# Attention and two expert layers on one core: gate rows of batch 0 in float32r from tiles of their own, later stacks in two tiles

## The chip, the cores and the metric

The kernel runs on one core of one Trainium2 chip. The metric is the time of one execution on the device in microseconds (us): the median of several runs. Lower is better. The engines are named as in the profile: PE is TensorE's matmul, PEld its weight load, DVE is VectorE, ACT ScalarE, POOL GpSimd and SP SyncE, which here only issues DMAs.

## The reference, cut to what matters

Attention over 4 batches of 8 heads, 576 positions and a head size of 64, with a causal mask and a bias from a running sum of `s`, and behind it two feed-forward layers on the 2304 tokens:

```python
scores = scale * np.matmul(q, k.transpose(0, 1, 3, 2))
s_pos = np.maximum(s, 0.0)
cum = np.cumsum(s_pos, axis=-1)
bias = -(cum[:, :, :, None] - cum[:, :, None, :])
scores = np.where(causal, -1000000000.0, scores + np.minimum(bias, 0.0))
attn = np.exp(scores - np.max(scores, axis=-1, keepdims=True))
attn = attn / (np.sum(attn, axis=-1, keepdims=True) + 1e-09)
out = np.matmul(attn, v)
# layer 1: h = x @ w_in; softmax of h times h; layer norm; @ w_out
# layer 2: h = x @ w_in; h * clip(h + 3, 0, 6) / 6; @ w_out
```

What matters here is the bias. It is a difference of two running sums, so a head's scores plus bias are one matrix product: the rows of q and k, and beside them four "gate rows" that hold the running sum in two parts (a float32r value and its rest) and ones.

## The kernel before, in words

**Tiling.** Two heads of a batch make a pair; pairs 0 to 3 are batch 0, pairs 4 to 15 the batches 1 to 3. Queries of a head are cut into five tiles t, of 128, 128, 128, 96 and 96 rows; a tile meets keys 0 to its own end, so its product is 128, 256, 384, 480 or 576 columns wide, the last as two pieces of 288. Each piece goes to one of eight PSUM banks, from there DVE (L525, with the mask and the row's minimum) writes it to SBUF, ACT takes the exponential (L537), POOL divides by the sum (L620, L638), PE transposes (L672), DVE or ACT copy back (L676) and PE multiplies with v (L701).

**Batch 0** (`qk_whole`, L577) runs in float32. For a tile it issues for both heads the product of the gate rows (m = 0) and then that of q and k (m = 1), each on 64 partitions, head 0 on partitions 0 to 63 and head 1 on 64 to 127. The gate rows lie in planes 2 and 3 of the tiles `whole0` and `whole1` (four planes of 576 columns; even pairs use `whole0`, odd ones `whole1`): rows 0 to 3 of each half hold gate rows, the others are zeros from one memset at the start (L286). Planes 0 and 1 take q and k of pairs 2 and 3; those of pairs 0 and 1 lie in `HL`. A pair's gate rows are loaded by `load_gates` (L421) from `rows_d`. Tiles 0 and 1 of all pairs come first (`pairs(False)`), then tiles 2 to 4 (`pairs(True)`).

**Batches 1 to 3** (`qk`, L604) run in float32r on 128 partitions, in two products a piece, from a stack per head parity (`stack0`, `stack1`, four planes): partitions 0 to 63 of planes 0 and 1 hold the high parts of q and k, partitions 64 to 127 of all four planes hold high and low parts, and rows 0 to 3 of planes 2 and 3 the gate rows. `to_stack` fills it by DMA on SP: for q and for k one copy of 64 x 576 (L485) and one of 64 x 2 x 576 (L486), then the gate rows (L489). A stack has one buffer, so the copies for a pair wait for the last product of that head parity in the pair before. The tags `stack0` and `stack1` first hold `whole0` and `whole1`; the stacks take their place, with a memset of planes 2 and 3 on POOL (L499).

**Around it.** PE also carries layer 1 (L806 with w_in, L872 the transposes, L893 with w_out) and, at the end, layer 2 (L1053, L1084). The weights come as float64 and are decoded on ACT, DVE and POOL between the steps of batch 0.

**The order.** Every step is added to a plan with an engine, a cost in us and what it reads and writes; the plan simulates the engines with these costs and gives each engine a fixed order. A cost in the plan is thus not a time on the chip but moves steps about, on every engine.

Of the kernel before, what the change touches and what calls it, by code (L numbers as in the profile page):

```python
# [184 lines left out]
def kernel(ctx, tc, q, k, v, s, w_in, w_out, g_ln, w2_in, w2_out, out):  # L185
    nc = tc.nc
# [71 lines left out]
    whole_t, stack_t = {}, {}  # L258
    nc.scalar.activation(out=nmax[:, 0, 0:1], in_=halfs, func=AF.Exp)

    def gate_rows():


        s_sb = ap2.tile([P, S], F32, tag="y4", name="s_sb")[:NH]
        one = ap2.tile([P, S], F32, tag="y4", name="one")[:NH]
        cum = ap2.tile([P, NQ, 2, D], F32, tag="V", name="cum").rearrange("p c j d -> p (c j d)")[:NH, :S]
        pos = ap2.tile([P, PT_COLS], F32, tag="pt", name="pos", bufs=PT).bitcast(F32R)[:NH, : 2 * S]
        neg = ap2.tile([P, PT_COLS], F32, tag="pt", name="neg", bufs=PT).bitcast(F32R)[:NH, : 2 * S]

        def load():  # L270
# [24 lines left out]
        for j in range(2):  # L295
            plan.add("POOL", 1.3, lambda j=j: zeros(j), writes=[f"zeros{j}"], new=[(f"stack{j}", 1, f"whole{j}")])

    def split64(plan, pool, src, hi, lo, name, key, scale=None, bufs=1, ring="", raws64=2, after=(), hi_dve=False, on_dve=(), behind=None):

# [112 lines left out]
            plan.add("SP", 0.5 + 0.5 * a, lambda j=j: values(j), writes=[f"{key}/{j}"], new=[("V", 2, key)] if j == 0 else [], lag=3.0, after=[begun(p)])  # L412

    def gates_at(p, j):
        return whole_t[p % 2][j * D : (j + 1) * D, 2:4, :]

    def load_gates(p, a):

        def gates():
            for j in range(2):  # L420
                nc.sync.dma_start(out=gates_at(p, j)[:4], in_=rows_d[2 * p + j].rearrange("i r s -> r i s"))  # L421

        plan.add("SP", 0.8, gates, reads=ROWS_D + [f"zeros{p % 2}", f"whole{p % 2}"], writes=[f"G{p}{a}"], new=[("G", 2, f"G{p}{a}")], lag=2.0)

    def prep_whole(p, name):

# [15 lines left out]

        if name == "q":
            load_gates(p, 0)
        ring = [("HL0", 2, hl_key)] if p < 2 else []
        home = [] if p < 2 else [f"zeros{p % 2}", f"whole{p % 2}"]
        for c0 in (0, 3):
            key = f"pp{p}{name}{c0}"
            plan.add("PE", 3 * 0.083, lambda c0=c0, key=key: turn(c0, key), reads=[raw_key, *home], writes=[key],
                     new=ring if name == "q" and c0 == 0 else [], bank=key, after=[] if name == "q" and c0 == 0 else [f"pp{p}q0"])  # L450
            plan.add(*(("ACT", act(3 * n)) if name == "q" else ("DVE", dve(3 * n))), lambda c0=c0, key=key: put(c0, key), reads=[key, *home], writes=[f"{hl_key}/{name}{c0}"])

    def prep_qk(p, name):
        if p < NPAIR:
# [42 lines left out]
        def zeros(j):  # L497
            stack_t[j] = ap1.tile([P, 4, S], F32R, tag=f"stack{j}", name=f"stack{j}")
            nc.gpsimd.memset(stack_t[j][:, 2:4, :].bitcast(F32), 0.0)  # L499

        def to_stack(j):
            if p == NPAIR and name == "q":
                plan.add("POOL", 1.3, lambda j=j: zeros(j), writes=[f"stack{j}/"], new=[(f"stack{j}", 1, f"stack{j}")])
            s_key = f"S{p}_{j}"
            plan.add("SP", 1.26, lambda j=j: stack(j), reads=[f"{hl_key}/{x}{c0}" for x in "hl" for c0, _ in groups] + [f"stack{j}/"],
                     writes=[f"{s_key}/{name}"], new=[(f"S{j}", 1, s_key)] if name == "q" else [], lag=3.0)
            if name == "k":
                plan.add("SP", 0.45, lambda j=j: gates(j), reads=ROWS_D + [f"stack{j}/"], writes=[f"{s_key}/g"], lag=2.0)
# [38 lines left out]
    def qk_whole(p, t):  # L547
# [32 lines left out]
        for c0, c1, at in pieces:  # L580
# [6 lines left out]
            plan.add("PE", 4 * max(0.07, 0.00033 * (c1 - c0)), lambda c0=c0, c1=c1, keys=keys: mm(c0, c1, keys),  # L587
                     reads=[f"HL{p}/{x}{c}" for x in "qk" for c in ((0, 3) if late else (0,))] + [f"G{p}{late:d}", f"whole{p % 2}"], writes=keys, new=new, bank=keys, after=[f"sc{heads[0]}_{t}_0"] if c0 else [])
# [6 lines left out]
    def qk(h, t):  # L595
# [587 lines left out]
```

## Time and profile before

| | |
|---|---|
| median of 3 runs | 851.12 us |
| lowest and highest | 850.43 and 853.88 us |
| the profiled execution | 855.06 us |
| its span | 853.1 us |
| PE busy | 822.0 us, 96% |
| DVE, ACT, POOL busy | 51%, 47%, 24% |
| L577, from first to last start | 15.2 to 90.4 us |
| L604, from first to last start | 98.4 to 362.5 us |
| shares of the chain that ended last, L577 and L604 | 3% and 5% |

The profile is one execution. Busy time of PE counts a matmul from its start to a modelled end, and matmuls overlap, so 96% does not say that PE is at its peak. A float32 product is two PE instructions in the trace. PEclk is the granted clock of TensorE as a share of 2.4 GHz; 0.50 is 1.2 GHz.

### The profile page before, as it was taken

What the parts mean: (1) busy time and instruction counts of PE and PEld (TensorE: products, weight loads), DVE (VectorE), ACT (ScalarE), POOL (GpSimd) and SP (SyncE); (2) the same over time, 40 slices, a digit from 0 to 9 for tenths busy, and PEclk for the clock granted to TensorE, in tenths of its full rate; (3) what the DMA queues carried; (4) which work ended last, traced back from release to release, by engine and by line L of the source; (5) the groups of instructions that cost most, each with busy time, mean ns of one, the idle gap of its engine ahead of it and who ended that gap; (6) DMA issues with size and microseconds to landing.
All of it is one profiled execution on the core that took longest, in us unless ns stands there. A gap on an engine that the chain in (4) does not pass through costs nothing.

```text
span 853.1 us, 13546 instructions
## 1 busy us (share of the span) xinstructions
PE 822.0 (96%) x4864; PEld 692.4 (81%) x4864; DVE 438.6 (51%) x1125; ACT 399.8 (47%) x928; POOL 206.0 (24%) x309
## 2 busy tenths in 40 slices
PE   3899999999999999998998999999999999999998
PEld 3565688988898889887897999998888888888886
DVE  4677887756756574658625894233222232222221
ACT  2575767756766566645534773243222322232222
POOL 1563644434533263335300221000000000000000
PEclk9899999999999999999999999999999999999999
DMA  6753596754556445243206660012000200010001
GB/s 171 179 148 110 126 210 148 174 129 109 127 138 136 101 103 123 63 136 107 86 32 202 203 219 1 0 62 87 1 0 1 87 13 0 1 50 1 0 1 50
DMA packets 95938, 77.52 MB, mean 91 GB/s; under 512 B 64288, under 2 KB 78112, under 8 KB 95872
## 3 DMA queue, kind: packets, MB, share of 16 engines
q1 hardware_dynamic: 93568, 68.27, 31.7%
q10 hardware_dynamic: 2304, 8.39, 3.0%
q8 instruction: 38, 0.62, 0.3%
q14 instruction: 28, 0.23, 0.1%
HBM read 45.38 MB, written 10.03 MB: 65 GB/s over the span
## 4 chain that ended last, share of the span: by engine, by line
PE 89%; DVE 4%; DMA 3%; POOL 2%; issue 1%; ACT 1%; SPq 0%; ACTq 0%; POOLq 0%; DVEq 0%
PE bank L1053 23%; PE bank L1084 23%; PE bank L893 11%; PE bank L806 10%; PE bank L701 6%; PE bank L672 5%; PE bank L604 5%; PE bank L577 3%; PE bank L872 2%; PE bank L467 1%; DMA raw_w2o<-in_moe_w_out_dram 1%; DMA stack<-HL12k 1%; POOL y L638 1%; DMA rows_d<-neg 1%; DVE y L525 0%
## 5 line engine op out<-in xcount | busy, mean ns | idle before, releaser
L1053 PE MATMUL bank<-x2h,w 128*128 128x512 f32 (+1 forms) x640 | 186.8, 373 | 0.5 <-ACT x2s L898 0.5
L1084 PE MATMUL bank<-w,gh 128*128 128x512 f32 x576 | 178.7, 393 | 2.1 <-ACT gh L1065 2.1
L1061 DVE SCALAR_TENSOR_TENSOR g<-g,bank 128x512 f32<-128x512 f32 (+1 forms) x80 | 50.6, 632 | 206.8 <-ACT g L1057 206.6
L1053 PEld LDWEIGHTS bank<-x2h,w 128*128 128x128 f32 x640 | 119.7, 189 | 19.4 <-ACT x2s L898 0.7
L1057 ACT ACTIVATE g<-bank 128x512 f32<-128x512 f32 (+1 forms) x80 | 44.4, 555 | 178.4 <-PE bank L1053 178.2
L1084 PEld LDWEIGHTS bank<-w,gh 128*128 128x128 f32 x576 | 107.9, 188 | 24.4 <-ACT gh L1065 2.5
L1053 PE MATMUL bank<-x2l,w 128*128 128x512 f32 (+1 forms) x320 | 119.1, 372 | 0.0
L1084 PE MATMUL bank<-w,gl 128*128 128x512 f32 x288 | 111.8, 392 | 0.0
L525 DVE CUSTOM_DVE_ANT_0 y<-bank,mask 96x288 f32<-96x288 f32 (+4 forms) x168 | 74.6, 467 | 56.9 <-PE bank L604 38.0
L537 ACT ACTIVATE y<-y,nmax 128x256 f32<-128x256 f32 (+4 forms) x140 | 83.4, 598 | 41.9 <-DVE nmax L525 29.9
L620 POOL TENSOR_SCALAR y<-y,rsum 128x128 f32<-128x128 f32 (+4 forms) x120 | 67.8, 583 | 101.8 <-DVE rsum L616 48.8
L893 PE MATMUL bank<-zh,w_out_h 128*128 128x256 f32 x288 | 82.9, 288 | 0.0
L893 PE MATMUL bank<-zl,w_out_h 128*128 128x256 f32 x288 | 81.2, 282 | 0.0
L893 PE MATMUL bank<-zh,w_out_l 128*128 128x256 f32 x288 | 81.2, 282 | 0.0
L1069 DVE TENSOR_TENSOR gl<-g,gh 128x512 fp32r<-128x512 f32 (+1 forms) x80 | 53.9, 674 | 41.5 <-ACT gh L1065 41.2
L1065 ACT CAST gh<-g 128x512 fp32r<-128x512 f32 (+1 forms) x80 | 46.2, 577 | 46.1 <-DVE g L1061 45.9
L1053 PEld LDWEIGHTS bank<-x2l,w 128*128 128x128 f32 x320 | 60.6, 189 | 8.3
L1084 PEld LDWEIGHTS bank<-w,gl 128*128 128x128 f32 x288 | 54.1, 188 | 12.0
L806 PE MATMUL bank<-w_in_h,xh 128*128 128x512 f32 x144 | 61.7, 429 | 0.8 <-DVE xh L788 0.8
L604 PE MATMUL bank<-stack 128*96 128x288 f32 (+4 forms) x288 | 57.8, 317 | 0.9 <-DMA stack<-HL12k 0.9
L806 PE MATMUL bank<-w_in_h,xl 128*128 128x512 f32 x144 | 57.7, 401 | 0.6 <-POOL xl L792 0.6
L806 PE MATMUL bank<-w_in_l,xh 128*128 128x512 f32 x144 | 57.7, 400 | 0.0
(220 smaller groups left out, 1359.6 us busy)
## 6 DMA issues: line engine op xcount, KB each, us to landing
raw_w2i<-in_moe_w_in_dram SPq DMA_DIRECT2D x16, 512.0 KB
raw_w2o<-in_moe_w_out_dram SPq DMA_DIRECT2D x16, 512.0 KB
rawq<-in_q_dram SPq DMA_DIRECT2D x32, 144.0 KB
rawk<-in_k_dram SPq DMA_DIRECT2D x32, 144.0 KB
x_d<-x2s SPq DMA_DIRECT2D x36, 128.0 KB
out_dram<-ob SPq DMA_DIRECT2D x18, 256.0 KB
raw_wi<-in_moe_w_in_dram ACTq DMA_DIRECT2D x8, 512.0 KB
raw_wo<-in_moe_w_out_dram ACTq DMA_DIRECT2D x8, 512.0 KB
```

The lines of the kernel that those rows point to most:

```text
L525: nc.vector.tensor_tensor_reduce(out=ys[h, t][:n, c0:c1], in0=bank(key)[:n, : c1 - c0], in1=mask[:n, 480 + n - w + c0 : 480 + n - w + c1], ...
L537: nc.scalar.activation(out=y[:n], in_=y[:n], func=AF.Exp, bias=nmax[:n, h, t : t + 1], scale=-1.0, accum_out=sums[:n, h, t : t + 1])
L604: nc.tensor.matmul(bank(key)[:n, : c1 - c0], lhsT=ss[:, 2 - 2 * m, ST[t] : w], rhs=ss[:, 3 - 2 * m, c0:c1], start=(m == 0), stop=(m == 1))
L620: nc.gpsimd.tensor_scalar(ys[h, t][:n], ys[h, t][:n], rsum[:n, h, t : t + 1], 1.0, ALU.mult, ALU.mult)
L701: nc.tensor.matmul(bank(key)[j * D : (j + 1) * D, lo - c0 : c1 - c0], lhsT=vs[v_key(p, a)][:n, jj, j, :], rhs=pts[pt_key(2 * p + j, a)][:n ...
L806: nc.tensor.matmul(bank(key), lhsT=xs[i][m // 2][:, kk, :], rhs=(w_in_l if m == 1 else w_in_h)[:, kk, f * 512 : (f + 1) * 512], start=(kk ...
L893: nc.tensor.matmul(bank(key)[:, : 2 * P], lhsT=w_out_at(w, kk)[:, m * P : (m + 1) * P], rhs=z[:, kk, :], start=(kk == 0 and i == 0), stop= ...
L1053: nc.tensor.matmul(bank(key)[:, :w], lhsT=wt[:, a, 0, c * P : (c + 1) * P], rhs=x[:, c, :w], start=(c == 0 and i == 0), stop=(c == KDM - 1 ...
L1061: nc.vector.scalar_tensor_tensor(out=gg, in0=gg, scalar=6.0, in1=bank(key)[:, :w], op0=ALU.min, op1=ALU.mult)
L1065: nc.scalar.copy(gh[:, :w], gg[:, :w])
L1069: nc.vector.tensor_sub(gl[:, :w], gg[:, :w], gh[:, :w].bitcast(F32))
L1084: nc.tensor.matmul(bank(key), lhsT=g_t[ci, m][1 + i // 2][:, t * P : (t + 1) * P], rhs=w2[m][:, i % 2, 1, :], start=(m == 0 and i == 0), s ...
```

## The change

The gate rows get tiles of their own, `gate0` and `gate1`, two planes each, of type float32r; the memset fills both planes once. `load_gates` and `gates_at` use them, so the gate products of batch 0 are float32r, the q k products stay float32. q and k of pairs 2 and 3 go to a tile of two planes under the tags `stack0` and `stack1`. The stacks of later batches keep planes 0 and 1 there; planes 2 and 3 are now `gate0` and `gate1`, whose rows below the gates are still zero, so the memset on POOL goes. The copy of 64 x 2 x 576 becomes two of 64 x 576, one to the stack and one to the gate tile. In the plan a stack's copies cost 1.6 us in place of 1.26, and a group of `qk_whole` 0.3 + 0.0007 us a column in place of four times 0.00033 a column (at least four times 0.07). All line numbers behind L455 move by up to four.

```diff
         def zeros(j):
-            whole_t[j] = ap1.tile([P, 4, S], F32, tag=f"stack{j}", name=f"whole{j}")
-            nc.gpsimd.memset(whole_t[j][:, 2:4, :], 0.0)
+            gate_t[j] = ap1.tile([P, 2, S], F32R, name=f"gate{j}")
+            nc.gpsimd.memset(gate_t[j].bitcast(F32), 0.0)
...
     def gates_at(p, j):
-        return whole_t[p % 2][j * D : (j + 1) * D, 2:4, :]
+        return gate_t[p % 2][j * D : (j + 1) * D, :, :]
...
-                hls[hl_key] = ap2.tile([P, 2, S], F32R, tag="HL", name=hl_key).bitcast(F32) if p < 2 else whole_t[p % 2][:, :2, :]
+                hls[hl_key] = ap2.tile([P, 2, S], F32R, tag="HL", name=hl_key).bitcast(F32) if p < 2 else ap1.tile([P, 2, S], F32, tag=f"stack{p % 2}", name=hl_key)
...
             nc.sync.dma_start(out=ss[:D, o, :].bitcast(F32), in_=hl[r, hi_at, :].bitcast(F32))
-            nc.sync.dma_start(out=ss[D:, o : o + 3 : 2, :].bitcast(F32), in_=hl[r, :, :].bitcast(F32))
+            nc.sync.dma_start(out=ss[D:, o, :].bitcast(F32), in_=hl[r, 0, :].bitcast(F32))
+            nc.sync.dma_start(out=gate_t[j][D:, o, :].bitcast(F32), in_=hl[r, 1, :].bitcast(F32))
...
-                plan.add("POOL", 1.3, lambda j=j: zeros(j), writes=[f"stack{j}/"], new=[(f"stack{j}", 1, f"stack{j}")])
+                plan.add("SP", 0.0, lambda: stack_t.update({j: ap1.tile([P, 2, S], F32R, tag=f"stack{j}", name=f"stack{j}")}), writes=[f"stack{j}/"], new=[(f"stack{j}", 1, f"stack{j}")])
+                plan.add("SP", 0.0, lambda: None, writes=[f"stack{j}/"], new=[("G", 2, f"G{p}{j}")])
...
-            plan.add("SP", 1.26, lambda j=j: stack(j), ...
+            plan.add("SP", 1.6, lambda j=j: stack(j), ...
...
-            plan.add("PE", 4 * max(0.07, 0.00033 * (c1 - c0)), lambda c0=c0, c1=c1, keys=keys: mm(c0, c1, keys),
+            plan.add("PE", 0.3 + 0.0007 * (c1 - c0), lambda c0=c0, c1=c1, keys=keys: mm(c0, c1, keys),
...
-            for m in range(2):
-                nc.tensor.matmul(bank(key)[:n, : c1 - c0], lhsT=ss[:, 2 - 2 * m, ST[t] : w], rhs=ss[:, 3 - 2 * m, c0:c1], start=(m == 0), stop=(m == 1))
+            for m, ss in enumerate((gate_t[h % 2], stack_t[h % 2])):
+                nc.tensor.matmul(bank(key)[:n, : c1 - c0], lhsT=ss[:, 0, ST[t] : w], rhs=ss[:, 1, c0:c1], start=(m == 0), stop=(m == 1))
```

Two places where the order moves. First PE, at the end of the first half of batch 0, from the last product with v of pair 3 (pt6a, pt7a) on; rawq4 and rawk4 are q and k of pair 4 to be transposed, xh0 and xl0 the two parts of the first token tile of layer 1. Before:

```order
L701 MATMUL bank5_101<-pt6a_496,V3a_420 64x128
L701 MATMUL bank5_101<-pt7a_501,V3a_420 64x128
L467 MATMUL bank0_96<-ident_60,rawq4_354 128x96 x3
L467 MATMUL bank2_98<-ident_60,rawq4_354 128x96 x3
L806 MATMUL bank5_101<-w_in_h_82,xh0_555 128x512
L806 MATMUL bank5_101<-w_in_l_83,xh0_555 128x512
L806 MATMUL bank5_101<-w_in_h_82,xl0_556 128x512
```

Now, from the transposes of rawq4 on (HL3 is q and k of pair 3, L574 the old L577, L802 the old L806):

```order
L466 MATMUL bank4_100<-ident_60,rawq4_356 128x96 x3
L466 MATMUL bank2_98<-ident_60,rawq4_356 128x96 x3
L466 MATMUL bank6_102<-ident_60,rawk4_391 128x96 x3
L466 MATMUL bank0_96<-ident_60,rawk4_391 128x96 x3
L574 MATMUL bank1_97<-gate1_134 96x480
L574 MATMUL bank7_103<-gate1_134 96x480
L574 MATMUL bank1_97<-HL3_346 96x480
L574 MATMUL bank7_103<-HL3_346 96x480
L574 MATMUL bank5_101<-gate1_134 96x288
L574 MATMUL bank3_99<-gate1_134 96x288
L802 MATMUL bank4_100<-w_in_h_82,xh0_577 128x512
```

Between the transposes of rawq4 and the first product of layer 1 there now stand those of rawk4 and two groups of pair 3 (of the second group the q k products are not shown, and they too stand ahead of layer 1); before, they stood far behind it.

Second SP, at the first stack of pair 4 (head parity 0). Before:

```order
L485 DMA stack0_825<-HL4q_543 64x576
L486 DMA stack0_825<-HL4q_543 64x2x576
L407 DMA V3b_863<-in_v_dram 128x3x64
L409 DMA V3b_863<-in_v_dram 96x2x64
L485 DMA stack0_825<-HL4k_767 64x576
L486 DMA stack0_825<-HL4k_767 64x2x576
L489 DMA stack0_825<-rows_d_71 4x2x576
```

Now:

```order
L484 DMA stack0_852<-HL4q_541 64x576
L485 DMA stack0_852<-HL4q_541 64x576
L486 DMA gate0_125<-HL4q_541 64x576
L407 DMA V3b_876<-in_v_dram 128x3x64
L409 DMA V3b_876<-in_v_dram 96x2x64
L484 DMA stack0_852<-HL4k_561 64x576
L485 DMA stack0_852<-HL4k_561 64x576
L486 DMA gate0_125<-HL4k_561 64x576
```

Three copies stand for q and for k where there were two, and the last of them, and later the gate rows, go to the gate tile.

## Rows read from the trace of the kernel before

**Rows 1.** The page, part 1: busy us, share of the span, instructions.

```profile
PE 822.0 (96%) x4864; PEld 692.4 (81%) x4864; DVE 438.6 (51%) x1125; ACT 399.8 (47%) x928; POOL 206.0 (24%) x309
```

**Rows 2.** Stretches: length, busy us (instructions) by engine, granted clock, DMA share, GB/s.

```profile
40.00:60.00 20.00, 17.52 (x102) 11.40 (x99) 16.97 (x62) 14.79 (x40) 12.78 (x16) 0.92 0.62 162
60.00:80.00 20.00, 20.00 (x132) 12.95 (x132) 15.21 (x34) 13.04 (x30) 10.36 (x14) 1.00 0.44 131
```

**Rows 3.** Chain that ended last, 14 to 62 us: start, us, what.

```profile
43.85 3.27 PE bank L577 x16
...
53.43 0.60 DVE a_wi L326
```

**Rows 4.** PE in order of time, groups of L577: start, us, line, tile<-source, shapes.

```profile
17.84 1.22 PE L577 MATMUL bank<-whole 64*128 64x256 f32 x4
18.85 1.06 PE L577 MATMUL bank<-HL 64*128 64x256 f32 x4
...
33.94 1.05 PE L577 MATMUL bank<-whole 64*96 64x480 f32 x4
34.82 0.97 PE L577 MATMUL bank<-HL 64*96 64x480 f32 x4
35.62 0.65 PE L577 MATMUL bank<-whole 64*96 64x288 f32 x4
36.11 0.65 PE L577 MATMUL bank<-HL 64*96 64x288 f32 x4
...
36.69 0.71 PE L434 MATMUL bank<-ident,rawk 96*128 96x96 f32 x6
```

**Rows 5.** PE in order of time, layer 1 between groups of L577.

```profile
80.69 0.51 PE L806 MATMUL bank<-w_in_h,xh 128*128 128x512 f32 x1
81.03 0.39 PE L806 MATMUL bank<-w_in_l,xh 128*128 128x512 f32 x1
81.27 0.40 PE L806 MATMUL bank<-w_in_h,xl 128*128 128x512 f32 x1
81.59 1.22 PE L577 MATMUL bank<-whole 64*96 64x288 f32 x8
```

**Rows 6.** PE in order of time, float32r products of L604, in narrow windows.

```profile
129.18 0.50 PE L604 MATMUL bank<-stack 128*128 128x256 f32 x2
...
129.30 0.60 PE L604 MATMUL bank<-stack 128*96 128x480 f32 x2
...
129.52 0.38 PE L604 MATMUL bank<-stack 128*96 128x480 f32 x1
```

**Rows 7.** PE in order of time, first products of layer 1; in brackets idle time and releaser.

```profile
54.88 0.50 PE L806 MATMUL bank<-w_in_h,xh 128*128 128x512 f32 x1 [0.80 <-DVE xh L788]
...
56.24 0.50 PE L806 MATMUL bank<-w_in_h,xl 128*128 128x512 f32 x1 [0.63 <-POOL xl L792]
```

**Rows 8.** Stretches of 2 us, columns as in rows 2.

```profile
24.00:26.00 2.00, 0.77 (x6) 0.40 (x5) 1.72 (x7) 1.48 (x6) 1.98 (x4) 0.99 0.41 96
...
28.00:30.00 2.00, 2.00 (x14) 1.70 (x14) 1.43 (x8) 0.63 (x2) 0.77 (x3) 0.50 0.43 127
...
56.00:58.00 2.00, 1.76 (x5) 1.43 (x6) 2.00 (x8) 0.93 (x3) 2.00 (x3) 0.67 1.08 316
58.00:60.00 2.00, 2.00 (x6) 1.52 (x6) 1.97 (x9) 1.99 (x6) 2.00 (x3) 0.50 1.14 181
```

**Rows 9.** SP's DMA issues in order of time: start, us, line, tile<-source.

```profile
89.77 0.48 SPq L485 DMA_DIRECT2D stack<-HL4k  x1
90.34 0.62 SPq L486 DMA_DIRECT2D stack<-HL4k  x1
```

**Rows 10.** POOL in order of time: the first stack's memset.

```profile
82.91 1.06 POOL L499 MEMSET stack<- 128x1152 f32 x1 [3.78 <-PE bank L577]
```

**Rows 11.** Waits of PE and of its weight loads: us in total, times, longest.

```profile
PE bank L604 <- DMA stack<-HL12k: 0.9, 1, 0.9
...
PEld bank L604 <- DMA stack<-rows_d: 1.1, 1, 1.1
```

**Rows 12.** PE in order of time: the first transposes of e.

```profile
90.77 1.09 PE L872 MATMUL bank<-ident,e 128*128 128x128 f32 x8
```

More of the change, by code (lines that the diff above doesn't have):

```diff
@@ L255 @@
     nc.gpsimd.affine_select(out=mask[:, 480:], in_=mask[:, 480:], pattern=[[-1, P]], compare_op=ALU.is_ge, fill=NEG, base=0, channel_multiplier=1)
-    whole_t, stack_t = {}, {}
+    stack_t, gate_t = {}, {}
     nc.scalar.activation(out=nmax[:, 0, 0:1], in_=halfs, func=AF.Exp)
@@ L295, in gate_rows @@
         for j in range(2):
-            plan.add("POOL", 1.3, lambda j=j: zeros(j), writes=[f"zeros{j}"], new=[(f"stack{j}", 1, f"whole{j}")])
+            plan.add("POOL", 1.3, lambda j=j: zeros(j), writes=[f"zeros{j}"])
     def split64(plan, pool, src, hi, lo, name, key, scale=None, bufs=1, ring="", raws64=2, after=(), hi_dve=False, on_dve=(), behind=None):
@@ L420, in gates @@
             for j in range(2):
-                nc.sync.dma_start(out=gates_at(p, j)[:4], in_=rows_d[2 * p + j].rearrange("i r s -> r i s"))
-        plan.add("SP", 0.8, gates, reads=ROWS_D + [f"zeros{p % 2}", f"whole{p % 2}"], writes=[f"G{p}{a}"], new=[("G", 2, f"G{p}{a}")], lag=2.0)
+                nc.sync.dma_start(out=gates_at(p, j)[:4].bitcast(F32), in_=rows_d[2 * p + j].rearrange("i r s -> r i s"))
+        plan.add("SP", 0.8, gates, reads=ROWS_D + [f"zeros{p % 2}"], writes=[f"G{p}{a}"], new=[("G", 2, f"G{p}{a}")], lag=2.0)
     def prep_whole(p, name):
@@ L444, in prep_whole @@
             load_gates(p, 0)
-        ring = [("HL0", 2, hl_key)] if p < 2 else []
-        home = [] if p < 2 else [f"zeros{p % 2}", f"whole{p % 2}"]
+        ring = [("HL0", 2, hl_key)] if p < 2 else [(f"stack{p % 2}", 1, hl_key)]
         for c0 in (0, 3):
             key = f"pp{p}{name}{c0}"
-            plan.add("PE", 3 * 0.083, lambda c0=c0, key=key: turn(c0, key), reads=[raw_key, *home], writes=[key],
+            plan.add("PE", 3 * 0.083, lambda c0=c0, key=key: turn(c0, key), reads=[raw_key], writes=[key],
                      new=ring if name == "q" and c0 == 0 else [], bank=key, after=[] if name == "q" and c0 == 0 else [f"pp{p}q0"])
-            plan.add(*(("ACT", act(3 * n)) if name == "q" else ("DVE", dve(3 * n))), lambda c0=c0, key=key: put(c0, key), reads=[key, *home], writes=[f"{hl_key}/{name}{c0}"])
+            plan.add(*(("ACT", act(3 * n)) if name == "q" else ("DVE", dve(3 * n))), lambda c0=c0, key=key: put(c0, key), reads=[key], writes=[f"{hl_key}/{name}{c0}"])
     def prep_qk(p, name):
@@ L485, in stack @@
             nc.sync.dma_start(out=ss[:D, o, :].bitcast(F32), in_=hl[r, hi_at, :].bitcast(F32))
-            nc.sync.dma_start(out=ss[D:, o : o + 3 : 2, :].bitcast(F32), in_=hl[r, :, :].bitcast(F32))
+            nc.sync.dma_start(out=ss[D:, o, :].bitcast(F32), in_=hl[r, 0, :].bitcast(F32))
+            nc.sync.dma_start(out=gate_t[j][D:, o, :].bitcast(F32), in_=hl[r, 1, :].bitcast(F32))
         def gates(j):
-            nc.sync.dma_start(out=stack_t[j][:4, 2:4, :].bitcast(F32), in_=rows_d[2 * p + j].rearrange("i r s -> r i s"))
+            nc.sync.dma_start(out=gate_t[j][:4, :, :].bitcast(F32), in_=rows_d[2 * p + j].rearrange("i r s -> r i s"))
         for c0, c1 in groups:
@@ L496, in prep_qk @@
             plan.add("DVE", dve(m), lambda c0=c0, c1=c1, key=key: low(c0, c1, key), reads=[key, f"{hl_key}/h{c0}"], writes=[f"{hl_key}/l{c0}"])
-        def zeros(j):
-            stack_t[j] = ap1.tile([P, 4, S], F32R, tag=f"stack{j}", name=f"stack{j}")
-            nc.gpsimd.memset(stack_t[j][:, 2:4, :].bitcast(F32), 0.0)
         def to_stack(j):
             if p == NPAIR and name == "q":
-                plan.add("POOL", 1.3, lambda j=j: zeros(j), writes=[f"stack{j}/"], new=[(f"stack{j}", 1, f"stack{j}")])
+                plan.add("SP", 0.0, lambda: stack_t.update({j: ap1.tile([P, 2, S], F32R, tag=f"stack{j}", name=f"stack{j}")}), writes=[f"stack{j}/"], new=[(f"stack{j}", 1, f"stack{j}")])
+                plan.add("SP", 0.0, lambda: None, writes=[f"stack{j}/"], new=[("G", 2, f"G{p}{j}")])
             s_key = f"S{p}_{j}"
-            plan.add("SP", 1.26, lambda j=j: stack(j), reads=[f"{hl_key}/{x}{c0}" for x in "hl" for c0, _ in groups] + [f"stack{j}/"],
+            plan.add("SP", 1.6, lambda j=j: stack(j), reads=[f"{hl_key}/{x}{c0}" for x in "hl" for c0, _ in groups] + [f"stack{j}/"],
                      writes=[f"{s_key}/{name}"], new=[(f"S{j}", 1, s_key)] if name == "q" else [], lag=3.0)
@@ L586, in qk_whole @@
                 new = [("wlate", 1, f"yl{p}")] if late else [("y2", 2, f"yf{h}") for h in heads]
-            plan.add("PE", 4 * max(0.07, 0.00033 * (c1 - c0)), lambda c0=c0, c1=c1, keys=keys: mm(c0, c1, keys),
-                     reads=[f"HL{p}/{x}{c}" for x in "qk" for c in ((0, 3) if late else (0,))] + [f"G{p}{late:d}", f"whole{p % 2}"], writes=keys, new=new, bank=keys, after=[f"sc{heads[0]}_{t}_0"] if c0 else [])
+            plan.add("PE", 0.3 + 0.0007 * (c1 - c0), lambda c0=c0, c1=c1, keys=keys: mm(c0, c1, keys),
+                     reads=[f"HL{p}/{x}{c}" for x in "qk" for c in ((0, 3) if late else (0,))] + [f"G{p}{late:d}"], writes=keys, new=new, bank=keys, after=[f"sc{heads[0]}_{t}_0"] if c0 else [])
             for h, key in zip(heads, keys):
```

1 line of the change is left out of this document (removed).

## The prediction

> **What bounds the kernel now.** I read the busy times and the granted clock first, then the busy time by stretches of 20 us, then the chain that ended last, then TensorE's order of time around the lines that change. TensorE (PE) is busy 96% of the span [rows 1]. From 60 to 80 us it is busy throughout, while the stretch from 40 to 60 us leaves it 2.5 us idle, with VectorE (DVE) at 17.0 of 20 us [rows 2]. So batch 0 has two halves with different limits. In its first half (about 15 to 56 us) the chain goes back and forth between the products of L577 and the softmax steps on DVE, ScalarE and GpSimd [rows 3]: a shorter L577 helps only until the next engine is late. In its second half (62 to 91 us) L577 stands between L806, L701 and L672 with no gap, and a nanosecond taken out there is a nanosecond earlier for what follows, which is again TensorE's work to the end of the span.
>
> **What a group of L577 costs now.** A group is one query tile of one pair: the gate products of two heads and the q k products of two heads, all in float32. At the upper clock level the gate part of 480 columns takes 34.82 - 33.94 = 0.88 us and the q k part 35.62 - 34.82 = 0.80 us; at 288 columns the two take 0.49 and 0.58 us [rows 4]. The cheapest reading is 0.80 / 480 = 1.67 ns a column for both heads together, that is four passes at 2.4 GHz, with the two heads side by side (one behind the other they would take twice that).
>
> **What it costs in float32r.** Before the change there is no float32r product with 64 rows, but L604 has float32r with 128 rows: two products of 256 columns start 0.12 us apart, two of 480 start 0.22 us apart [rows 6]. 0.22 / 480 = 0.46 ns a column, one pass. If the heads still run side by side, a column of the gate part falls from 1.67 to 0.46 ns, a saving of 1.21 ns; if they run one after the other it is 1.67 - 0.92 = 0.75 ns. I take side by side, since the float32 rows show it for the same operand positions. A pair has 128 + 256 + 384 + 480 + 288 + 288 = 1824 columns, four pairs 7296.
>
> **What it adds on TensorE.** The gate part is now of another type than the q k part behind it, and than the float32 work that often stands ahead. The trace prices such a change of type: between groups of L577, the first product of an L806 triple takes 81.03 - 80.69 = 0.34 us to the next start, the second 0.24, and the third 0.32 up to L577 [rows 5]. So entering float32r costs about 0.10 us and leaving it about 0.08, 0.18 us for both. A group that stands behind L806 pays nothing new, since the boundary was there already.
> But in those rows two things change at once, the type and the rows of the array (128 to 64), and no row shows a change of type alone; between gate and q k part only the type changes. That is a rival below.
> The Trainium skill, TensorEngine Tiling (Array Packing), Key Properties, says that changing the tiling mode drains TensorE; by that rule alone the gate and q k parts, both on 64 rows, need no drain between them.
>
> **The sum.**
> Second half, 62 to 91 us: eight groups with 2 x 384 + 2 x 480 + 4 x 288 = 2880 columns, 2880 x 1.21 = 3.5 us saved. In the new order three of the eight stand right behind L802 (the old L806), five behind float32 work: 5 x 0.18 = 0.9 us lost. Net 2.6 us, wholly on the path.
> First half: sixteen groups, 4416 columns, 5.3 us, less 16 x 0.18 = 2.9 us, makes 2.4 us. Two stretches run at the lower level, where a pass costs twice as much: from 28 to 30 us the granted clock is 0.50 [rows 8], and at the start the gate part of 256 columns takes 18.85 - 17.84 = 1.01 us [rows 4], though the clock column shows nothing there. The groups of 128 and 256 columns in both (768 columns) give a further 768 x 1.21 = 0.9 us: 3.3 us. Of the sixteen, five lie off the chain (1056 columns, 1.3 - 0.9 = 0.4 us), so 2.9 us lie on it. Against it stands DVE at 85% of 40 to 60 us [rows 2]. I take two thirds, 1.9 us; the bounds are 0 and 3.3.
> The gap at 54 to 56 us: TensorE waits 0.80 us for xh and 0.63 us for xl ahead of the first L806 [rows 7], and then falls to the lower level: 0.67 from 56 to 58 us and 0.50 from 58 to 60 us [rows 8] are some 1.3 + 2.0 us at half speed, 1.7 us of work lost. In the new order the transposes of rawk for pair 4 and two groups of pair 3 (480 and 288 columns) stand in this place, nearly 3 us of work that stood far behind these products before. It could fill the gap if its banks and inputs are free: between 0 and 1.4 + 1.7 = 3.1 us. I take 1.0, because this work too needs DVE to empty its banks.
> The stacks of batches 1 to 3: a copy of 64 x 576 takes 0.48 us of SP's issue time and the one of 64 x 2 x 576 took 0.62 [rows 9]; the latter becomes two of the former, so a head's q and k copies take 2 x (2 x 0.48 - 0.62) = 0.7 us longer, 24 heads. SP has room, and bytes stay the same. It costs time only where TensorE waits for a stack: it did so twice, 0.9 and 1.1 us [rows 11]. Bounds: 0, and 2 us if those two double; I take 0.5. Queued behind these copies on SP are the next loads of V, q and k, which are issued a step ahead of use. The two fills of zeros that GpSimd did for the stacks go (1.06 us each) [rows 10], and GpSimd waited for rsum before its next work of that kind, so I cost that at nothing; were that cover gone, it would be a gain of 1 us or less.
> Steps of the plan that only record an order (SP at 0.0 us) issue nothing. Memory stays the same: two tiles of two rows in place of one of four.
> Total: 2.6 + 1.9 + 1.0 - 0.5 = 5.0 us. The profiled execution took 855.06 us (span 853.1 and 2.0 around it), so a like execution would take 850.1. That execution is 3.9 us above the median of the timed runs, 851.12, and I move the difference over: **846.1 us**.
>
> **Rivals.**
> *The first half gives nothing* (chance 0.20). DVE, ScalarE and GpSimd work through their queues in order, interleaved with the decoding of w_in, and a faster L577 only makes them the limit at once. For it: 17.0 of 20 us of DVE [rows 2]. Against it: the chain there carries groups of L577 as long as 3.27 us in a piece [rows 3]. Then 2.6 - 0.5 = 2.1 us remain: 849.0.
> *The heads' float32r products do not run side by side* (0.07): the change would do half of what it says. 7296 x 0.46 = 3.4 us are lost, two thirds of that on the path, 2.3: 848.4.
> *The change of type is free* (0.08). If the 0.18 us belong to the change from 128 to 64 rows of the array alone, the second half keeps its 0.9 us and the first two thirds of its 2.9: 2.8 us more gain, 843.3. For it: the two are mixed in every boundary of the trace [rows 5]. Against it: the boundary between two parts of one group, where neither changes, is not free either (0.88 us for 480 columns against 0.80 [rows 4]). This is what the rule of the Trainium skill on tiling modes, above, would make of it.
> *The clock* (0.10). TensorE fell to the lower level after the two stretches in which it had least to do: from 24 to 26 us it was busy for 0.77 of 2 us [rows 8], and from 54 to 56 us it waited [rows 7]. With less work in the first half there are more such gaps. Each stretch like that ahead of 60 us costs 1.7 us; two more of them eat 3.4 of the 5.0: 849.5. The Trainium skill, TensorE: Matmul & The Clock Gate, What's actually happening, says the same of the direction: the clock follows how busy the array has been; the trace agrees with the direction.
> *Slower: the stacks arrive late* (0.06). Each head's stack is a single buffer: its copies wait for the last product of the same head parity of the pair before, and the next products wait for the copies. If two thirds of the 24 heads turn out to be waiting for the third copy, 16 x 0.7 = 11.2 us are lost against 5.0 gained: 857.3. From about seven heads on (7 x 0.7 = 4.9) nothing of the gain is left, and from fourteen on (9.8 - 5.0 = 4.8) the kernel is slower by over 0.5%. Against it: only two heads wait now [rows 11].
>
> **How the numbers follow.** The forecast has a chance of 0.49. A measurement of this kernel can tell about 0.5%, 4.26 us, from no change: 846.86 and 855.38 are the marks. The forecast lies just beyond the first, and its own spread (first half 0 to 3.3, gap 0 to 3.1, stacks 0 to 2) reaches from 842.1 (2.6 + 3.3 + 3.1 = 9.0) to 850.5. I put 0.37 of its 0.49 beyond the mark, since the gap and the lower clock can give more than I took, with it the free change of type (0.08) and 0.05 of the other rivals: faster 0.50. Slower has 0.06 from the stacks and 0.02 for the changed order, which moves work on every engine from 30 to 350 us. The rest, 0.42, is within 0.5%. The range from 842.0 to 852.0 leaves out the late stacks and a few ends.
>
> **What would show it.** In the profile after: gate rows of 288 columns whose pair takes 0.12 to 0.15 us at the upper level, and a step of about 0.1 us ahead of each q k part (else the type change or the side by side was read wrongly); L577's busy time between 62 and 91 us down by some 3 us; the transposes of e (L872, at 90.77 us now [rows 12]) 4 to 6 us earlier; no wait of TensorE between 54 and 56 us; waits for stacks of no more than 3 us in total. It would be wrong if the transposes of e come earlier and the end does not, which would point at the stacks or at a new wait between 90 and 360 us, or if they do not come earlier at all, which would point at DVE or the clock.

## The result, and the profile after

The changed kernel takes **860.19 us** (median of 4 runs, 859.03 to 860.80); the kernel before, run beside it, 850.90. The ratio is 1.0100, with a 95% interval of 1.0074 to 1.0126: slower by 1%. The prediction was 846.1 us with a range of 842.0 to 852.0, so both the sign and the range were wrong. The profiled execution of after took 860.80 us, its span 858.8.

The page of after, part 1, and its stretches of 20 us (columns: length, busy us and instructions of PE, PEld, DVE, ACT and POOL, granted clock, DMA share, GB/s), as [rows 1, 2]:

```profile
PE 819.4 (95%) x4816; PEld 689.3 (80%) x4816; DVE 441.2 (51%) x1125; ACT 400.0 (47%) x928; POOL 205.1 (24%) x307
```

```profile
20.00:40.00 20.00, 14.60 (x80) 9.92 (x78) 10.21 (x39) 10.45 (x33) 6.33 (x10) 0.83 0.70 166
40.00:60.00 20.00, 17.16 (x110) 11.48 (x111) 18.23 (x66) 14.23 (x38) 12.80 (x16) 0.84 0.60 166
60.00:80.00 20.00, 15.44 (x83) 10.36 (x79) 15.10 (x23) 9.23 (x19) 10.84 (x12) 0.73 0.44 133
```

From 60 to 80 us PE was busy throughout before, at a clock of 1.00 [rows 2]; now it stands idle for 4.6 us and the granted clock is 0.73. The products themselves do what was hoped. PE in order of time, as [rows 4, 5, 12]:

```profile
79.00 0.45 PE L574 MATMUL bank<-gate 64*128 64x384 f32 x2
79.29 0.81 PE L574 MATMUL bank<-HL 64*128 64x384 f32 x4
80.02 0.51 PE L802 MATMUL bank<-w_in_h,xh 128*128 128x512 f32 x1
...
87.23 0.40 PE L802 MATMUL bank<-w_in_h,xl 128*128 128x512 f32 x1
87.55 0.37 PE L574 MATMUL bank<-gate 64*96 64x288 f32 x2
87.77 0.65 PE L574 MATMUL bank<-HL 64*96 64x288 f32 x4
...
99.08 1.03 PE L868 MATMUL bank<-ident,e 128*128 128x128 f32 x8
```

The gate part of 288 columns is now 87.77 - 87.55 = 0.22 us, where it was 0.49 [rows 4]. But the first transposes of e start at 99.08 us instead of 90.77 [rows 12]. That 8.3 us late start is most of the loss of 9.3 us; at the last transposes of e the two traces are 10.0 us apart.

Where PE waited, in the whole span (the last row is from the kernel before, where L577 waited once for gate rows):

```profile
PE bank L574 <- DMA gate<-rows_d: 12.8, 2, 8.4
PE bank L434 <- POOL gate L286: 4.9, 1, 4.9
PE bank L868 <- POOL e L843: 4.6, 2, 4.2
PE bank L802 <- DVE HL4q L478: 4.6, 1, 4.6
...
PE bank L577 <- DMA whole<-rows_d: 8.1, 1, 8.1
```

Before, that wait was at the start, and the first product of layer 1 waited 0.80 [rows 7]. So two waits are new: 12.8 - 8.4 = 4.4 us for a gate load, and 4.6 us of layer 1 for HL4q. The chain that ended last shows what stands behind each (start, us, what):

```profile
27.02 4.32 DMA raw_wi<-in_moe_w_in_dram
31.35 0.31 SPq L389
31.76 4.05 DMA gate<-rows_d
35.81 0.14 issue
35.95 2.86 PE bank L574 x6
...
57.06 5.20 POOL y L634 x6
62.26 1.24 POOL w_in_l L342
63.52 0.68 ACT a_wo L318
64.22 0.63 DVE a_wo L326
64.85 0.90 issue
65.74 0.46 DVE HL4q L478
66.24 1.65 PE bank L802 x3
```

**First stall, 31.5 to 36 us.** The gate load of the late tiles was issued at 31.76 us, because SP, which issues it, was held up in the copy of rawk ahead of it by a load of weights (raw_wi) on another queue. **Second stall, 61.7 to 66.2 us.** The first product of layer 1 waits for its bank, which still holds the transposes of pair 4; DVE empties it (HL4q) only behind the decoding of w_out (a_wo), and that waits, through a buffer, for a low part of w_in on POOL, which stands behind six scalings of y. Around both the granted clock is 0.50 (1.2 GHz) for some us. These two were my first theory.

For what follows I add up, over the 48 stretches of 2 us from 14 to 110 us, PE's idle time (2 us less its busy time) and the work lost at the lower clock level (busy time x (1 - granted clock)). Before: 7.7 and 5.0 us, 12.7 together. After: 17.0 and 7.9, 24.9 together.

### The profile page after: what moved, and what is told of

It is laid out like the page before. It is cut to its first block, busy times and chain, and to the rows that moved or that the text cites. A ratio compares the mean times of both kernels' runs of the same rounds, so it can differ in the third digit from the quotient of the medians.

```text
span 858.8 us, 13535 instructions
## 1 busy us (share of the span) xinstructions
PE 819.4 (95%) x4816; PEld 689.3 (80%) x4816; DVE 441.2 (51%) x1125; ACT 400.0 (47%) x928; POOL 205.1 (24%) x307
## 4 chain that ended last, share of the span: by engine, by line
PE 88%; DMA 3%; DVE 3%; POOL 2%; issue 1%; ACT 1%; SPq 1%; POOLq 0%; DVEq 0%; ACTq 0%
PE bank L1049 23%; PE bank L1080 23%; PE bank L889 12%; PE bank L802 11%; PE bank L697 5%; PE bank L600 5%; PE bank L668 5%; PE bank L868 2%; PE bank L574 2%; PE bank L466 1%; DMA gate<-rows_d 1%; POOL y L634 1%; DMA rawq<-in_q_dram 1%; DMA rows_d<-neg 1%; DMA xr<-x_d 1%
## 5 line engine op out<-in xcount | busy, mean ns | idle before, releaser
L534 ACT ACTIVATE y<-y,nmax 128x384 f32<-128x384 f32 (+4 forms) x140 | 83.5, 597 | 40.3 <-DVE nmax L522 33.7
L802 PE MATMUL bank<-w_in_h,xh 128*128 128x512 f32 x144 | 62.5, 434 | 5.5 <-DVE HL4q L478 4.6
L802 PE MATMUL bank<-w_in_h,xl 128*128 128x512 f32 x144 | 57.9, 402 | 0.8 <-POOL xl L788 0.8
L802 PE MATMUL bank<-w_in_l,xh 128*128 128x512 f32 x144 | 57.9, 402 | 0.0
L889 PEld LDWEIGHTS bank<-zh,w_out_h 128*128 128x128 f32 x288 | 54.6, 190 | 1.2 <-issue 0.3
```

The costliest lines, as they stand in the source:

```text
L534: nc.scalar.activation(out=y[:n], in_=y[:n], func=AF.Exp, bias=nmax[:n, h, t : t + 1], scale=-1.0, accum_out=sums[:n, h, t : t + 1])
L802: nc.tensor.matmul(bank(key), lhsT=xs[i][m // 2][:, kk, :], rhs=(w_in_l if m == 1 else w_in_h)[:, kk, f * 512 : (f + 1) * 512], start=(kk ...
L889: nc.tensor.matmul(bank(key)[:, : 2 * P], lhsT=w_out_at(w, kk)[:, m * P : (m + 1) * P], rhs=z[:, kk, :], start=(kk == 0 and i == 0), stop= ...
```

## Experiments

**Code and order apart.** Four kernels. `x1`: the changed code, with the planner's entries as before, so that every instruction and bank stands in the old order:

```diff
-            plan.add("PE", 0.3 + 0.0007 * (c1 - c0), ...
+            plan.add("PE", 4 * max(0.07, 0.00033 * (c1 - c0)), ...
-            plan.add("SP", 1.6, lambda j=j: stack(j), ...
+            plan.add("SP", 1.26, lambda j=j: stack(j), ...
# and the reads of load_gates, prep_whole and the groups again with whole0 / whole1
```

`x2`: the code of before with the changed entries, so in the new order. `x4`: x1 with the gate products in float32:

```diff
-                    a, b = (hl[:, 0, :], hl[:, 1, :]) if m else (g[:, 0, :], g[:, 1, :])
+                    a, b = (hl[:, 0, :], hl[:, 1, :]) if m else (g[:, 0, :].bitcast(F32), g[:, 1, :].bitcast(F32))
```

`e_oldcosts`: the changed kernel with the two old costs alone (first diff without its last line).

> The changed code (one-pass gate products, tiles of their own, two-tile stacks with their third copy) with every instruction in the order, and every result in the bank, of the kernel before; only the two clears of the stacks are gone from POOL. If the new order costs the time (my theory), this runs at 845 to 849 us, which is what the prediction's terms for the gate products give without the order's. If the code costs it (change of type on PE, third copy, a lower clock), it runs at 855 us or more. First transposes of e (L868 of the changed kernel): 85 to 88 us by the first, 95 us or later by the second.

> The code of the kernel before (four-pass gate products, four-plane tiles, clears on POOL) with every instruction in the order and every result in the bank of the changed kernel. If the order costs the time: 862 to 868 us, since the two stalls of the changed kernel (4.4 and 4.6 us, and the half clock behind them) stand here too, and nothing is saved on the gate products. If the code costs it: 850 to 853 us, and no PE wait over 2 us between 30 and 70 us.

> The tiles of their own and the two-tile stacks with the third copy, in the order of the kernel before, but the gate products stay in float32 with their four passes. If the order is the cause: 850 to 852.5 us, as the kernel before, so that the third copy costs at most 1.5 us. If the split is the cause: 855 us or more. The difference to the kernel with the one-pass products in the same order is what these alone are worth: 4 to 5 us by the prediction, 0 or less by the rival.

> The changed kernel with the planner's two costs put back (a group of gate and q k products as before, the stack copies at 1.26): it plans as if the products still took four passes, so that only the dependences of the changed code move the order. If the shorter cost of a group is what makes the bad order: 846 to 851 us, with no wait of over 2 us for a gate load near 32 us or for xh near 62 us. If the changed dependences (the clears gone from POOL, the gates no longer tied to the stacks) make it: 856 to 862 us, with one of these stalls or both.

| | code before | changed code |
|---|---|---|
| order before | 851.86 us | x1: **845.76** us, 0.9928 (0.9909 to 0.9948) |
| new order | x2: 859.68 us, 1.0095 (1.0070 to 1.0119) | 860.19 us, 1.0100 (1.0074 to 1.0126) |

x4 takes 848.55 us (0.9967, 0.9950 to 0.9984), e_oldcosts 855.37 (1.0038, 1.0020 to 1.0056). The code gains 6.1 us in the old order; the order loses 7.8 with the old code and 14.4 with the new. In the new order the code brings nothing. x2 waits as the changed kernel does at the second stall (PE waits, 0 to 110 us), and it lost 17.4 us in idle time and clock, the changed kernel 24.9: the 7.5 us more eat up all that the code gains. Of them 5.5 us lie from 30 to 44 us (8.2 against 2.7), at the first stall, which x2 does not have: SP issued its gate load at 28.22 us, not held by raw_wi. The first stall thus does not come with the new order alone, and the expectation that both would stand in x2 was wrong there.

```profile
PE bank L806 <- DVE HL4q L478: 3.6, 1, 3.6
PE bank L577 <- DVE nmax L525: 2.4, 2, 1.9
```

x1 lost 12.8 us by the same count, as much as the kernel before (12.7), and kept its gain. Busy time of L577 from 62 to 91 us, x4 and then x1:

```profile
62.00:91.00 29.00, 11.44 (x64) 1.00 0.38 102
```

```profile
62.00:91.00 29.00, 7.90 (x48) 1.00 0.44 118
```

That is 3.5 us less, and the first transposes of e are 89.94 - 87.27 = 2.7 us earlier (x4, x1; layer 1 itself starts 0.3 us earlier):

```profile
89.94 1.09 PE L871 MATMUL bank<-ident,e 128*128 128x128 f32 x8
```

```profile
87.27 1.09 PE L871 MATMUL bank<-ident,e 128*128 128x128 f32 x8 [0.57 <-POOL e L846]
```

The two profiled executions took nearly the same time, 848.38 us (x4) and 848.10 (x1, its slowest run): behind a gap of PE near 386 us, which both have, x1 fell to 0.50 and lost 2.8 us of work, x4 stayed at 1.00. What the gate products are worth is therefore read from the medians, 2.8 us, and not from these two spans.

x2's first transposes of e come at 98.6 us. So the theory "the new order costs the time" held in its signs and in x1; x2 came out 2.3 us under its range, and x4 was 3.3 us faster than the kernel before, where I had put 850 to 852.5; the 2.8 us from x4 to x1 lie between the two forecasts for it (4 to 5 us, and 0 or less). e_oldcosts fell between its two forecasts, 0.6 us under the second and 9.6 us behind x1, which has the same code and the same prices: the changed dependences too make a worse order. (Its expectation calls the new cost of a group the shorter one. It is the higher one at every width: 0.39 us for 0.28 at 128 columns, 0.50 for 0.38 at 288, nearly equal at 480.) Layer 1 comes early there (transposes of e at 86.31), and then PE waits 2.41 us for the gate rows of the first stack and falls to half speed (its granted clock is 0.50 from 92 us on):

```profile
88.00:90.00 2.00, 0.18 (x2) 0.21 (x2) 1.11 (x1) 1.44 (x4) 1.72 (x2) 1.00 0.85 196
...
92.00:94.00 2.00, 2.00 (x14) 1.77 (x14) 1.50 (x4) 1.62 (x5) 1.71 (x3) 0.50 0.91 208
```

**The two stalls one by one.** In the changed kernel, steps of the plan are moved after the planning, by giving them another time:

```diff
+MOVES = {
+    ('ACT', 'raw_wi3_0'): 24.5,          # y2, y12: three instructions later on ACT
+    ('POOL', 'xs0/l'): 45.75,            # y1, y12: xl ahead of the six scalings
+    ('ACT', 'HL4q/h0'): 48.5,            # y1, y12: and h3, HL4k, and on DVE the low parts
...
-        for _, i in sorted(order):
+        for _, i in sorted((moved.get(i, t), i) for t, i in order):
```

`z1` is x1 with the first of these moves. The reason for it stands in the built program: eight completion semaphores (counters by which a DMA reports that it is done) are handed out to the DMAs in turn, across the queues, and an issue waits until the DMA that had its semaphore last is done. In the changed kernel the load raw_wi3 on ACT's queue and the second copy of rawk of pair 3 on SP's have the same one (first row ACT, others SP):

```
L312 DMA raw_wi3_0_323<-in_moe_w_in_dram 128x1024 [waits DMAHW5_49,Activation_49]
L389 DMA rawk3_292<-in_k_dram 96x6x64 [waits DMAHW4_49,PE_49]
L389 DMA rawk3_292<-in_k_dram 96x6x64 [waits DMAHW5_49]
```

In the kernel before, raw_wi3 had the next one (DMAHW6). The second copy of rawk3 waits for DMAHW5 there too, but for an earlier DMA that had it; SP's longest wait for a DMA from 20 to 40 us is 0.3 us. In the built programs of x2 and x4 raw_wi3 has DMAHW6 as well, in that of x1 DMAHW5.

> The changed kernel with nine of its steps put earlier: xl of the first row tile ahead of the six scalings of y on POOL, and the high and low parts of pair 4 (HL4q, HL4k) ahead of the decoding of w_out on ACT and DVE, so that the banks that they hold come free early. Theory (the stall before the first product of the second stage, 4.56 us, and the half clock behind it are about half the loss): 852 to 856 us, and the wait of that product for HL4q is under 1 us. Rival (whatever fills the gap, another engine is the bound there and the wait moves on): 858 to 861 us.

> The changed kernel with one step put later: the issue of the load raw_wi3 on the queue of ACT, by three instructions, so that in the round of eight completion semaphores, which are handed out in turn, it no longer shares one with the second copy of rawk of pair 3 on the queue of SP. Theory (SP was held 4.0 us by that shared semaphore, and the gate load behind it came 4.4 us late): the wait for the gate load near 32 us falls from 4.4 to under 1.5 us, SP is held by raw_wi nowhere ahead of it, and the time is 854 to 858 us. Rival (the gate load is late for another reason): the wait stays over 3 us and the time is 859 to 861 us.

> Both moves together in the changed kernel. Theory (the two stalls with the half clock behind them are nearly all of the loss): 846 to 851 us. Rival (the new order loses in many small places): 853 us or more.

> The changed code in the order of the kernel before, where SP was also held by raw_wi (3.1 us, PE waited 1.67 us for the gate load and then ran at half clock from 34 to 37 us), with the issue of raw_wi3 put later in the same way. If the shared semaphore costs there too: 842 to 845 us, 1 to 3 us less than without the move. If that wait is covered on the way to the end: 845 to 847 us, no difference.

| | us | ratio | PE idle and lost to the clock, 14 to 110 us |
|---|---|---|---|
| y1 | 860.80 | 1.0086 (1.0060 to 1.0113) | 19.1 + 5.1 |
| y2 | 857.48 | 1.0055 (1.0035 to 1.0076) | 18.8 + 4.3 |
| y12 | 858.30 | 1.0069 (1.0050 to 1.0088) | 16.7 + 6.8 |
| z1 | 847.77 | 0.9944 (0.9925 to 0.9964) | 11.2 + 1.7 |

The mechanism of the first stall is right: in y2 SP issued the gate load at 27.50 us instead of 31.76, and the wait near 32 us is gone.

```profile
26.53 0.87 SPq L395 DMA_DIRECT2D rawk<-in_k_dram  x2
27.50 0.71 SPq L427 DMA_DIRECT2D gate<-rows_d  x2
32.62 0.39 SPq L413 DMA_DIRECT2D V2a<-in_v_dram  x1
```

Now SP is held by raw_wi ahead of V2a instead, for 4.4 us, the next gate load is late (2.43 us of wait at 42.38 us), and the wait for HL4q grows from 4.6 to 6.2 us. The time fell by 2.7 us, into its forecast, though the two intervals still touch. The second stall is another matter: y1 took the wait for HL4q away, and the kernel was as slow as without the move, as its rival had it, since PE then waited 4.4 us for pt0b. y12 was not 846 to 851 us but 858.3; my theory of two stalls fell. Its waits of PE from 54 to 80 us:

```profile
PE bank L683 <- DVE pt0b L687: 2.9, 1, 2.9
PE bank L589 <- DVE nmax L537: 1.9, 1, 1.9
PE bank L683 <- POOL y L649: 1.1, 1, 1.1
PE bank L817 <- DVE HL4q L493: 0.3, 1, 0.3
```

z1 shows no gain over x1 (2.0 us more, above both of its forecasts, with intervals that overlap). In x1 the hold of SP (3.1 us) made the gate load late; in z1 the gate load is in time, and SP is held by raw_wi for 4.7 us ahead of V2a. So the late gate load cost the old order nothing that reaches the end; an order without any hold was not run.

**One more step along the same wait.** `y3` is y12 with the decoding of the first three tiles of w_out put behind the copies of pt0b and pt1b (17 more entries in MOVES).

> The kernel with both moves (858.3 us), and the decoding of the first three tiles of w_out put behind the copies of the transposes pt0b and pt1b on ACT and DVE, where the kernel before has it. Reason: in the kernel with both moves ACT waited 2.7 us in its first a_wo for a low part of w_in on POOL, DVE waited behind it, and PE waited 2.9 us for pt0b, whose copy stood behind. Theory (what is queued behind the decoding of w_out on ACT and DVE makes the loss in the second half of batch 0, wherever PE meets it first): the wait for pt0b falls under 1 us, PE stands idle under 4 us from 54 to 70 us instead of 6.1, and the time is 850 to 854 us. Rival (the new order has too little work for PE there whatever stands on ACT and DVE): the wait moves on once more, idle stays over 5 us, and the time is 857 to 860 us.

It took 859.48 us (1.0082, 1.0069 to 1.0095). PE's idle time from 54 to 70 us did fall, from 6.1 to 2.1 us, so the theory's own sign came; but from 70 to 86 us it rose from 1.4 to 4.8, with waits for pt2b in place of pt0b:

```profile
PE bank L606 <- DVE pt2b L704: 2.4, 1, 2.4
PE bank L606 <- DVE nmax L554: 1.9, 1, 1.9
PE bank L700 <- DVE nmax L554: 1.4, 1, 1.4
```

The rival held: the wait moves on. In this order PE meets, from 54 to 86 us, one step after another that needs ACT, DVE and POOL just then. x1 shows what the old order has there: the first product of layer 1 stands at 53.75 us, and from 55.45 to 59.63 us PE runs six of its triples of products without a gap, work that waits for nobody while the others catch up.

**Which part of the change makes the order.** `c3`: x1 with the two new costs and nothing else. `c_late`: x1 with the new cost of a group on the late halves alone. `t_trueprice`: x1 with a group priced as its trace shows.

```diff
-            plan.add("PE", 4 * max(0.07, 0.00033 * (c1 - c0)), ...
+            plan.add("PE", 0.3 + 0.0007 * (c1 - c0), ...                # c3; c_late: only if late
+            plan.add("PE", 0.48 + 0.0015 * (c1 - c0), ...               # t_trueprice
-            plan.add("SP", 1.26, ...
+            plan.add("SP", 1.6, ...                                     # c3 alone
```

> The kernel of the changed code in the old order, with nothing changed but the planner's two costs (a group of gate and q k products at 0.3 us and 0.7 ns a column, the stack copies at 1.6): the dependences stay those of the kernel before. Its first 129 rows on PE then stand as in the changed kernel. If the new costs alone bring the bad order: 857 to 862 us. If it takes the changed dependences too: 846 to 854 us.

> The same, with the new cost of a group on the late halves of the pairs alone; the early halves and the stack copies keep the old costs. If the re-pricing of the early halves is what turns the order (by the trace all of the loss up to 54 us lies there, but only some 5 of 12 us): 848 to 854 us. If the late halves turn it (the first product of the second stage stands behind the late groups of pair 3 and the transposes of pair 4): 855 us or more.

> The changed code in the old order's plan, with one thing changed: a group of gate and q k products is priced as the trace of that kernel shows it, 0.48 us and 1.5 ns a column (0.67 us from start to next at 128 columns, 1.02 at 384, 1.19 at 480), where the old plan has 0.28 to 0.63 and the changed one 0.39 to 0.64. If the order is bad because its prices are wrong: 840 to 846 us, at or below the 845.8 of the old order. If the old order is one good draw of a planner that goes step by step, and any re-pricing is another draw: 848 to 858 us.

| | us | ratio |
|---|---|---|
| x1, old prices | 845.76 | 0.9928 (0.9909 to 0.9948) |
| t_trueprice | 847.76 | 0.9955 (0.9940 to 0.9970) |
| c_late | 855.55 | 1.0040 (1.0024 to 1.0055) |
| c3, new prices | 861.15 | 1.0123 (1.0100 to 1.0146) |

c3 shows that the new prices alone, on the changed code, are enough for all of the loss. They are not the only way to it: e_oldcosts, with the old prices and the changed dependences, lost 9.6 us against x1. The first product of layer 1 waits in c3 as in the changed kernel:

```profile
66.25 0.80 PE L805 MATMUL bank<-w_in_h,xh 128*128 128x512 f32 x1 [5.75 <-DVE HL4q L479]
```

c_late came out at the lower edge of its second forecast, between x1 and c3: the late halves make part of the loss, and what the early halves and the stack copies add was not run by itself. t_trueprice fell between its forecasts, 1.8 us above the first and 0.2 below the second; its interval overlaps that of x1. The loss is thus not the lot of any re-pricing. A price that follows the chip gave an order about as good as the old one; the new price gave a bad one. Why, these runs do not say beyond this: of a group's 0.67 us at 128 columns, 1.02 at 384 and 1.19 at 480 (x1's trace), the new price has 0.39, 0.57 and 0.64, so it understates them by a factor of 1.7 to 1.9; but the old one does so by 1.9 to 2.4 and gave the best order. The plan's own end, which the kernel computes as it is built and which is no time of the chip, ranks x1, t_trueprice, e_oldcosts, c_late, the changed kernel and c3 as their medians on the chip do. It contains the prices themselves, so the rank is no test; but that the first of its three plans ends 6.7 us later on PE in the changed kernel than in the kernel before (359.6 against 352.9 us) could have been read beforehand.

The version that beats both kernels is x1: 845.76 us, 0.7% under the kernel before.

## Why the prediction was wrong, step by step

- **The step that failed: the changed order.** The prediction knew that a cost in the plan "moves steps about, on every engine", counted what the new order puts at 54 to 56 us as a possible filling, +1.0 us, and gave all else 0.02 of a chance "for the changed order". Measured, with the code held: 7.8 us (x2) to 14.4 us (the changed kernel against x1) lost, where the sum has a gain of 1.0. The sum was made as if the instructions stayed in their places.
- **The gap at 54 to 56 us** (+1.0, bounds 0 to 3.1): wrong in sign, outside its bounds. The two groups of pair 3 waited 1.85 us themselves for DVE, and the transposes of rawk held two more banks; layer 1 went from 54.88 [rows 7] to 66.24 us. The order rows in the section on the change showed the new neighbours; what they did not show, and I did not ask, is who empties their banks and when: `HL4q` stood behind the decoding of w_out on ACT and DVE.
- **Gate products, second half** (2.6 us net, "wholly on the path"): the size is near, its terms are not. In the old order L577's busy time there fell by 11.44 - 7.90 = 3.5 us, what 2880 x 1.21 gave, without the 0.9 us for the change of type. And not all of it reached the path: x1's lead over x4 grew from 0.9 us at the first layer 1 product behind 62 us to 2.7 us at the transposes of e, since x1 waited 0.8 us for xl and 0.6 us for e, which x4 did not. Timed, x4 to x1, the one-pass products are worth 848.55 - 845.76 = 2.8 us in all.
- **Side by side** (0.46 ns a column): right. The gate part of 288 columns takes 0.22 us where 288 x 0.46 = 0.13 are columns, that of 384 columns 0.29 where 0.18 are.
- **The change of type** (0.18 us a group): not there. The step of 0.1 us ahead of the q k part came as forecast, but it is not the type's. x4 has the same products in float32 throughout:

```profile
80.44 0.40 PE L805 MATMUL bank<-w_in_h,xl 128*128 128x512 f32 x1
80.77 0.73 PE L577 MATMUL bank<-gate 64*96 64x288 f32 x4
81.33 0.65 PE L577 MATMUL bank<-HL 64*96 64x288 f32 x4
```

  Its gate part takes 81.33 - 80.77 = 0.56 us, 288 x 1.67 = 0.48 and 0.08 more, where the float32r part has 0.22 - 0.13 = 0.09 more. From the last product of layer 1 to the gate part it is 0.33 us in x4, where the type changes, and 0.32 in the changed kernel (87.23 to 87.55), where it does not; between two products of layer 1 it is 0.24 [rows 5]. So the rival "the change of type is free", which had 0.08, was right on the mechanism, though the time was not the one that it gave. The Trainium skill, TensorEngine Tiling (Array Packing), Key Properties, ties a drain to a change of tiling mode; the trace agrees as far as it goes: the step into the gate part, where the rows go from 128 to 64, is the same with and without a change of type.
- **First half** (1.9, bounds 0 to 3.3): next to nothing. In x1 layer 1 starts 54.06 - 53.75 = 0.3 us before that of x4; part of this may be the late gate load that x1 has and x4 has not, but z1, where it is in time, starts layer 1 only 0.1 us earlier and is no faster. The rival that put 0 there was the better reading.
- **Stacks** (-0.5, bounds 0 to 2, and the rival of late stacks): no loss seen. x4 has the third copy, with the tiles of their own and without the memsets, and is 3.3 us faster than the kernel before; the copy was not run by itself. The wait of L604 for a stack, 0.9 us [rows 11], does not occur in x4 or x1. Of the rest only the place is known: x4 leads by 0.8 us at the first transposes of e, by 1.9 at 160 us and by 4.0 at the last ones. Of these, 1.4 us are work that the kernel before lost at the lower clock from 390 to 396 us, behind the gap that x4 has too; the rest was not tested.
- **The clock rival**: in the changed kernel it is real, 7.9 us of work lost to 110 us against 5.0 before, but as a follower of the stalls.
- **The 3.9 us moved over** from the profiled execution to the median: right. In that trace PE waited 2.1 us for gh in layer 2, at 464 us, and then lost 1.7 us at the lower clock; no other trace has a wait of over 0.8 us there.
- By luck, **the forecast of 846.1 us fits x1**, the change in the old order: 845.76. Its terms were 2.6 + 1.9 + 1.0 - 0.5; measured, they were 2.8 for the gate products and 3.3 for the rest of the code.

## What to carry to other kernels

Where a planner sets the order, a change of its prices, or of what a step reads and writes, is a change of the whole program: keep the old order for a first run of new code, and then re-plan as a second change, measured by itself. Ahead of a prediction, follow the new order at the places where PE is about to wait: which bank an instruction gets, which step empties that bank, and what stands ahead of that step on its engine. And when a wait is taken out and the next one takes its place, as in y1, y12 and y3, look for the cause in the order and not in the wait.

## What the runs showed of the hardware that was not expected

- **A DMA issue on one queue can wait for a DMA of another** through a shared completion semaphore: 4.0 us on SP, for a load that ACT had issued. In the built programs, who shares follows from the order of all DMAs, so it comes and goes with edits that touch no DMA: x4 and x1 differ in the type of the gate products alone, and only x1 has the hold. The waits of SP's queue in x1, 20 to 40 us:

```profile
SPq L389 <- DMA raw_wi<-in_moe_w_in_dram: 3.1, 1, 3.1
```

- **A dip of the same size need not bring the lower clock.** Before, PE was busy for 0.77 of 2 us from 24 to 26 us, and from 26 us on the granted clock was 0.50 [rows 8], 1.2 GHz; x4 has a dip of the same size and stays at 1.00 (first row the kernel before, the others x4):

```profile
26.00:28.00 2.00, 1.89 (x11) 1.46 (x9) 0.47 (x2) 1.67 (x6) 1.80 (x2) 0.50 0.58 131
...
24.00:26.00 2.00, 0.80 (x7) 0.43 (x6) 1.73 (x6) 1.61 (x6) 1.85 (x4) 1.00 0.32 69
26.00:28.00 2.00, 1.68 (x15) 1.25 (x15) 0.95 (x4) 1.64 (x6) 1.94 (x2) 1.00 0.74 162
28.00:30.00 2.00, 2.00 (x23) 1.47 (x20) 1.52 (x10) 1.53 (x6) 1.23 (x4) 1.00 0.52 132
```

  So an estimate of a stretch at half speed from one execution, as the 1.7 us in the prediction, is good for that execution only. The mean granted clock of one and the same kernel differs too: from 0.990 to 0.998 in the 23 runs of the kernel before that stood beside x1.
